# Triangular inverses of a delta-rule attention in other pieces, and their round trip through HBM at other places

## The chip, the cores and the metric

The kernel runs on one core of a Trainium2 chip. The metric is the device time of one execution in microseconds (us). The kernel before took 492.99 us (median of three runs, 492.59 to 494.81).

## What is computed

Two layers. The first is a linear attention with the delta rule, over 4 batches and 8 heads, 768 tokens each, head size 48, all in float32:

```
state = 0                                     # 48 x 48 per batch and head
for t in range(768):
    y[t]  = q[t] @ state
    state = state + beta[t] * outer(k_n[t], v[t] - k_n[t] @ state)     # k_n: k over its norm
```

The second takes the 3072 tokens of width 384 (8 heads of 48), sends each to the best of 8 experts (softmax of a gate, argmax), and multiplies the weight of that expert with `relu(x @ w1[e]) @ w2[e]` (384 to 1024 to 384).

## The kernel before, in words

**Attention, the part that is changed.** The 768 tokens are cut into 6 blocks of 128 (`tb` = 0 to 5). One *item* n = 4 tb + b is block tb of batch b with its 8 heads, so there are 24 items. The program is written as 27 *ticks* t (the loop at L1030): in tick t item t enters, the items t-1 to t-3 move one stage of 32 tokens on, and item t-3 is finished. Every tick has the same steps on TensorE (PE): `residual` (L439, L451), `apply` (L466), `finish` (L489, L500, L509), the products with the queries (`qpart`, L280, tile pq), the Gram matrix of the keys of a later item (`kpart`, L280, tile pg, up to tick 11 only), and the product that hands a finished item to the experts (L533). VectorE (DVE) subtracts the residual (`v_all<-v_all,ks`, L458) once per tick. That instruction stands between `residual` and `apply` of its tick; below, *tick t lasts from the start of L458 of t to that of t+1*.

**Inverses.** The 32 x 32 sub-blocks need, for all 4 batches, 8 heads and 4 stages of a block, the inverse of a unit lower triangular matrix built from the Gram matrix. One 32 x 32 matrix lies on each of 128 partitions, in `lg` (the products) and `lw` (the inverse). DVE does this alone. `prepare` (L310) scales, `lanes` (L362) inverts the two 16 x 16 triangles on the diagonal column by column, c = 1 to 14, with one multiply (L379) and one add (L382) for both triangles at once through a 4-dimensional view (`both_halves`), and then forms the 16 x 16 corner from two products, each as multiply (L398) and reduce (L404) in three pieces of 4, 5 and 7 rows through two buffers `big0` and `big1`. A transpose (L409) gives `wt`, which `apply` of the block's four items reads. The inverse of block 0 stands ahead of tick 0; that of block tb must be done before tick 4 tb, and what is left of it is then put in at one go:

```
while line and line[0].tb <= t // B:
    inverse_step(t)
```

Otherwise the steps of the inverses are strewn over the ticks: each `yield` of `lanes` names a cost in us, and `beside(t, i)`, called seven times a tick, puts in steps up to a budget (`SPEND`, 0.86 to 0.92 us). `ROOT[tb]` gives the places 7t+i at which block tb has its squared norms taken (`squares`, L304, DVE), their square root (`root`, L308, ScalarE, ACT) and at which its inverse may start.

**The round trip.** The Gram of an item lies in `gg` with tokens on partitions; `lg` wants one matrix per partition. So, when the fourth item of a block is through `kpart`, SyncE (SP) stores four slices to HBM (`gd`, L268) and loads the block back as `lg` (L272). For blocks 2 to 5 that is in the middle of tick max(0, 4 tb - 9). SP issues all other loads too, in the order of the program: keys (`kt`, L196), queries, values (`v_all`, L228, L230), and seven clears of the token table in HBM (`xg<-zrow`, L191, 788 KB each, their places set by `CL` and `CLT`). The load of `lg` waits until the stores of `gd` have landed.

**Experts.** From tick 20 on the weights are loaded and split, and behind tick 26 eight experts are computed, on PE at 2.4 GHz almost without a break. This part is not changed.

Of the kernel before, what the change touches and what calls it, by code (L numbers as in the profile page):

```python
# [41 lines left out]
def deltanet_moe(ctx, tc, kt_d, qt_d, kn_d, v_d, beta_d, w_gate, w1, w2, out):  # L42
# [81 lines left out]
    ROOT = {1: (-1, -1, -1), 2: (17, 20, 22), 3: (38, 41, 43), 4: (66, 69, 71), 5: (94, 97, 99)}  # L124
# [9 lines left out]
    CL = (1, (0, 1), (0, 1))  # L134
    CLT = (2, 3, 4, 5)
# [98 lines left out]
    def kpart(n):  # L234
# [28 lines left out]
        if tb > 0 and b == B - 1:  # L263
            early_ = CL[tb] if tb < len(CL) else (0, 0)
            clear_slots(early_[0])
            for i in range(NB):
                r = slice(32 * i, 32 * i + 32)
                nc.sync.dma_start(out=gd[tb].rearrange("(i n) (r c) -> i r n c", i=NB, r=32)[i],  # L268
                                  in_=gg_g[tb % (KSL // B)].rearrange("p b h c -> p (b h) c")[r, :, r])
            tiles[tb]["lg"] = fp.tile([128, 32, 32], F32, name=f"lg{tb}", tag="lg", bufs=3)  # L270
            clear_slots(early_[1])
            nc.sync.dma_start(out=tiles[tb]["lg"].rearrange("p r c -> p (r c)"), in_=gd[tb])  # L272
# [37 lines left out]
    def prepare(tb):  # L310
# [50 lines left out]

    def lanes(tb):  # L362


        T = tiles[tb]
        lg, lw = T["lg"], T["lw"]
        G, W = both_halves(lg), both_halves(lw)
        V = nc.vector
        tmp = fp.tile([128, 128], F32, name=f"tmp{tb}", tag=f"tmp{tb % 2}")
        for c in range(15):  # L370
            m, w = 15 - c, c + 1
            if c == 0:
                for g in (0, 16):
                    V.tensor_scalar(out=lw[:, g + 1:g + 16, g], in0=lg[:, g + 1:g + 16, g], scalar1=lw[:, g, g:g + 1],
                                    scalar2=None, op0=ALU.mult)
                yield 0.4
                continue
# [16 lines left out]
        todo = []  # L394
        for i, (x, y, out, minus) in enumerate(work):
            m, n, k = x.shape[1], y.shape[1], x.shape[2]
            t = big[i % 2][:, 0:m * n * k].rearrange("p (m n k) -> p m n k", m=m, n=n)
            V.tensor_tensor(out=t, in0=x.unsqueeze(2).broadcast_to([128, m, n, k]),  # L398
                            in1=y.unsqueeze(1).broadcast_to([128, m, n, k]), op=ALU.mult)
            yield 0.15 + m * n * k / 960  # L400
            todo.append((out, t, minus))
            while len(todo) > (i not in (2, 5)):
                out, t, minus = todo.pop(0)
                V.tensor_reduce(out=out, in_=t, axis=AX.X, op=ALU.add, negate=minus)  # L404
                yield 0.15 + t.shape[1] * t.shape[2] * t.shape[3] / 960
# [623 lines left out]
    fin = iter(())  # L1029
    for t in range(NN + LAG):  # L1030
# [345 lines left out]
```

## Time and profile before

| what | value |
|---|---|
| median of the runs | 492.99 us |
| profiled execution: time / span | 495.15 us / 493.4 us |
| busy share of the span: PE, DVE, ACT, POOL | 91%, 66%, 54%, 34% |
| the inverse of block 0 on DVE, L341 to L409 | from 12.10 to 36.57 us |
| L458 of tick 0, 12, 20 starts at | 36.42, 140.69, 201.67 us |
| last L458 (tick 26) | 256.06 us |
| mean granted clock of TensorE | 0.975 |

The rows further down come from the profiled execution; times in them count from its span's start. A row of a timeline gives start, length, engine, line, operation, output and inputs with their shapes, the number of instructions merged, and in brackets how long the engine was idle before it and what released it.

### The profile page before, as it was taken

How to read it: one execution, taken by the hardware profiler on the slowest of the kernel's cores; microseconds unless marked ns; L12 is line 12 of the kernel's file. 1: busy time of each engine (PE TensorE's matmuls, PEld its weight loads, DVE VectorE, ACT ScalarE, POOL GpSimd, SP SyncE). 2: the span in 40 equal slices, each digit the busy share in tenths (PEclk: the TensorE clock that was granted, in tenths of full speed). 3: DMA queues.
4: the chain of work that ended last, by engine and by line, in shares of the span. 5: the costliest groups of instructions: out<-in, count | busy, mean ns of one | idle time of the engine just before them, and what ended most of it. 6: DMA issues, size and time to landing. Idle time of an engine off the chain costs nothing. (4 is left out here: it accounts for less than half of the span.)

```text
span 493.4 us, 17242 instructions
## 1 busy us (share of the span) xinstructions
PE 451.3 (91%) x7212; PEld 417.2 (85%) x7212; DVE 326.3 (66%) x728; ACT 264.7 (54%) x580; POOL 166.8 (34%) x342
## 2 busy tenths in 40 slices
PE   6979597989998898987899899999999999999995
PEld 4868486878887777876798899999999999999995
DVE  5999798699999989556543687373563637265230
ACT  4467385667666565777342465463554545364230
POOL 7002142667887878731301210201112020201111
PEclk9698798999999999999999999999999999999999
DMA  8599649667284433635211557374544547353101
GB/s 241 169 273 231 169 95 273 196 131 202 84 169 118 132 107 92 214 126 188 81 55 45 168 171 247 119 217 136 173 142 166 165 160 211 118 177 98 38 1 46
DMA packets 57147, 73.33 MB, mean 149 GB/s; under 512 B 25929, under 2 KB 44831, under 8 KB 57056
## 3 DMA queue, kind: packets, MB, share of 16 engines
q1 hardware_dynamic: 53600, 62.44, 43.7%
q0 software_dynamic: 3456, 9.57, 5.3%
q8 instruction: 71, 1.16, 1.0%
q14 instruction: 20, 0.16, 0.1%
HBM read 54.15 MB, written 18.62 MB: 147 GB/s over the span
## 5 line engine op out<-in xcount | busy, mean ns | idle before, releaser
L808 POOL DMA_INDIRECT out_dram<-yo,idx x32 | 30.8, 963 | 199.3 <-ACT yo L1146 103.5
L805 PE MATMUL y<-w2h,hx 128*128 128x384 f32 x352 | 93.5, 340 | 0.1
L751 DVE TENSOR_TENSOR w2l<-w2r,w2h 128x768 fp32r<-128x768 f32 x32 | 31.2, 979 | 68.8 <-ACT w2h L749 68.7
L805 PEld LDWEIGHTS y<-w2h,hx 128*128 128x128 f32 x352 | 64.1, 188 | 0.4 <-issue 0.4
L805 PE MATMUL y<-w2l,hx 128*128 128x384 f32 x176 | 59.3, 337 | 0.0
L794 PE MATMUL h<-xl,w1h 128*128 128x416 f32 (+2 forms) x168 | 57.3, 341 | 0.2 <-DVE xl L726 0.2
L794 PE MATMUL h<-xh,w1h 128*128 128x416 f32 (+2 forms) x168 | 57.3, 341 | 0.0
L794 PE MATMUL h<-xh,w1l 128*128 128x416 f32 (+2 forms) x168 | 57.2, 341 | 0.0
L470 ACT COPY u<-ks 32x384 f32<-32x384 f32 x96 | 45.1, 470 | 18.3 <-PE ks L466 16.8
L797 ACT ACTIVATE hx<-h 128x448 fp32r<-128x448 f32 (+1 forms) x64 | 32.8, 518 | 31.7 <-PE h L794 31.0
L1146 ACT ACTIVATE yo<-y,gt 128x384 f32<-128x384 f32 x22 | 12.8, 582 | 68.4 <-PE y L805 56.9
L798 DVE SCALAR_TENSOR_TENSOR hx<-h,hx 128x448 fp32r<-128x448 f32 (+1 forms) x64 | 37.1, 587 | 16.2 <-ACT hx L797 16.2
L280 PE MATMUL pg<-kt 64*128 64x128 f32 x384 | 35.9, 315 | 12.8 <-DMA kt<-in_kt_dram 7.2
L291 POOL TENSOR_SCALAR_AFFINE_SELECT pm<-pm 128x1024 f32<-128x1024 f32 x24 | 27.8, 1159 | 51.9 <-ACT pm L290 51.5
L439 PE MATMUL ks<-st,kt 128*32 128x96 f32 x768 | 43.5, 251 | 0.3 <-ACT u L470 0.2
L280 PEld LDWEIGHTS pg<-kt 64*128 64x128 f32 x384 | 30.1, 213 | 16.0 <-DMA kt<-in_kt_dram 6.1
L262 ACT COPY gg<-pg 128x512 f32<-128x512 f32 x48 | 25.7, 587 | 24.9 <-PE pg L280 24.9
L541 POOL DMA_INDIRECT xg<-row,sli x24 | 28.3, 1178 | 23.6 <-ACT yt L513 8.0
L439 PEld LDWEIGHTS ks<-st,kt 128*32 128x32 f32 x768 | 32.6, 110 | 3.9 <-ACT u L470 0.7
L751 DVE TENSOR_TENSOR w1l<-w1r,w1h 128x1024 fp32r<-128x1024 f32 x24 | 29.4, 1223 | 8.9 <-ACT w1h L749 8.9
L466 PE MATMUL ks<-v_all,wt 32*32 32x48 f32 x1536 | 25.0, 205 | 10.5 <-DVE v_all L458 6.3
L466 PEld LDWEIGHTS ks<-v_all,wt 32*32 32x32 f32 x1536 | 21.0, 106 | 14.7 <-DVE v_all L458 8.1
(196 smaller groups left out, 1041.7 us busy)
## 6 DMA issues: line engine op xcount, KB each, us to landing
w1r<-in_w_dram SPq DMA_DIRECT2D x24, 512.0 KB
w2r<-in_w_dram SPq DMA_DIRECT2D x32, 384.0 KB
xg<-zrow SPq DMA_DIRECT2D x7, 788.0 KB
kt<-in_kt_dram SPq DMA_DIRECT2D x17, 256.0 KB
xr<-xg SPq DMA_DIRECT2D x7, 591.0 KB
ku<-in_kn_dram SPq DMA_DIRECT2D x20, 192.0 KB
qt<-in_qt_dram SPq DMA_DIRECT2D x36, 96.0 KB
v_all<-in_v_dram SPq DMA_DIRECT2D x15, 192.0 KB
```

The lines of the kernel that those rows point to most:

```text
L280: nc.tensor.matmul(pg[a][:, p], lhsT=kt[r, p], rhs=xt[r, p], start=True, stop=True, tile_position=(64 * a, 0), skip_group_check=True)
L291: nc.gpsimd.affine_select(out=pm, in_=pm, compare_op=ALU.is_gt, fill=0.0, base=0, pattern=[[0, H], [1, C]], channel_multiplier=-1)
L439: nc.tensor.matmul(ks[32 * q:32 * q + 32, 2 * p:2 * p + 2, :], lhsT=kt_t[n % KTL][:, p, 32 * q:32 * q + 32], rhs=st_view(n % B, p), start= ...
L466: nc.tensor.matmul(ks[r, h, :], lhsT=tiles[n // B]["wt"][r, n % B * H + h, :], rhs=vn[r, h, :], start=True, stop=True, tile_position=(32 * ...
L470: nc.scalar.copy(out=uview(n)[r], in_=ks[r])
L541: put = nc.gpsimd.indirect_dma_start(out=xg, out_offset=bass.IndirectOffsetOnAxis(ap=at, axis=0), in_=x, in_offset=None, bounds_check=OFF ...
L751: nc.vector.tensor_tensor(out=lo[:, j:j + st], in0=raws[k], in1=hi[:, j:j + st].bitcast(F32), op=ALU.subtract)
L794: nc.tensor.matmul(ps, lhsT=w[:, d, fs], rhs=x_[:, d], start=(n == 0), stop=(n == len(terms) - 1))
L797: nc.scalar.activation(out=hh, in_=ps, func=AF.Relu)
L798: nc.vector.scalar_tensor_tensor(out=hl, in0=ps, scalar=0.0, in1=hh.bitcast(F32), op0=ALU.max, op1=ALU.subtract)
L805: nc.tensor.matmul(ps, lhsT=h(f)[h_], rhs=w2[w][:, f, :], start=(n == 0), stop=(n == len(terms) - 1))
L808: nc.gpsimd.indirect_dma_start(out=out, out_offset=bass.IndirectOffsetOnAxis(ap=idx, axis=0), in_=yo, in_offset=None, bounds_check=N - 1, ...
```

## The change

Three parts. (1) In `lanes` each triangle gets a chain of its own: where one multiply and one add did both triangles, there are now two multiplies (one for the matrix at 0, one for that at 16) and then two adds, for c = 1 to 13; the last column is one fused multiply-add per triangle. `prepare` leaves the diagonal and the last column out of its scaling (15 x 15 for 16 x 16). (2) The corner's products come in four pieces of 4 rows each, in the order 0, 1, 3, 2, pieces 1 and 3 side by side in `big1`. The costs that the steps name to the budget are changed with them. (3) For blocks 2 to 5 the stores of `gd` move to the end of their tick, and the load of `lg` to the end of the next tick, ahead of its `load_k`; one clear of `xg` that stood between them moves to the end of tick 1 (`CLT`). `ROOT` lets the blocks start 4 or 5 places later.

```
-    ROOT = {1: (-1, -1, -1), 2: (17, 20, 22), 3: (38, 41, 43), 4: (66, 69, 71), 5: (94, 97, 99)}
+    ROOT = {1: (-1, -1, -1), 2: (22, 25, 27), 3: (42, 45, 47), 4: (70, 73, 75), 5: (98, 101, 103)}
...
-    CL = (1, (0, 1), (0, 1))
-    CLT = (2, 3, 4, 5)
+    CL = (1, (0, 1), (0, 0))
+    CLT = (1, 2, 3, 4, 5)
...
-            x = lg[:, g:g + 16, g:g + 16]
+            x = lg[:, g + 1:g + 16, g:g + 15]
...
-        for c in range(15):
+        for c in range(1, 14):
             m, w = 15 - c, c + 1
-            x = tmp[:, 0:2 * m * w].rearrange("p (g a b) -> p g a b", g=2, a=m)
-            V.tensor_tensor(out=x, in0=G(w, c, m, 1).broadcast_to([128, 2, m, w]),
-                            in1=W(c, 0, 1, w).broadcast_to([128, 2, m, w]), op=ALU.mult)
-            yield 0.2 + m * w / 480
-            V.tensor_tensor(out=W(w, 0, m, w), in0=W(w, 0, m, w), in1=x, op=ALU.add)
-            yield 0.2 + m * w / 480
+            x = [tmp[:, i, 0:m * w].rearrange("p (a b) -> p a b", a=m) for i in range(2)]
+            for i, g in ((0, 0), (1, 16)):
+                V.tensor_tensor(out=x[i], in0=lg[:, g + w:g + 16, g + c:g + w].broadcast_to([128, m, w]),
+                                in1=lw[:, g + c:g + w, g:g + w].broadcast_to([128, m, w]), op=ALU.mult)
+            yield 0.2 + m * w / 700
+            for i, g in ((0, 0), (1, 16)):
+                y = lw[:, g + w:g + 16, g:g + w]
+                V.tensor_tensor(out=y, in0=y, in1=x[i], op=ALU.add)
+            yield 0.2 + m * w / 700
+        for g in (0, 16):
+            y = lw[:, g + 15, g:g + 15]
+            V.scalar_tensor_tensor(out=y, in0=lw[:, g + 14, g:g + 15], scalar=lg[:, g + 15, g + 14:g + 15], in1=y,
+                                   op0=ALU.mult, op1=ALU.add)
...
-        for a, b in ((0, 4), (4, 9), (9, 16)):
-            work.append((first_[:, a:b, a:16], lg[:, 16:32, a:16], prod[:, a:b], False))
-        for a, b in ((12, 16), (7, 12), (0, 7)):
-            work.append((lw[:, 16 + a:16 + b, 16:16 + b], prod[:, :, 0:b], lw[:, 16 + a:16 + b, 0:16], True))
+            for i in (0, 1, 3, 2):
+                a = 4 * i if up else 12 - 4 * i
+                if up:
+                    x, y, out = left[:, a:a + 4, a:16], lg[:, 16:32, a:16], prod[:, a:a + 4]
+                else:
+                    x, y, out = lw[:, 16 + a:20 + a, 16:20 + a], prod[:, :, 0:a + 4], lw[:, 16 + a:20 + a, 0:16]
...
+        if crossing:
+            bounce_in(crossing.pop())
         load_k(t + LEAD + 2)
         if t >= LAG:
             load_q(t - LAG + QTL)
+        for tb in range(2, NT):
+            if t == max(0, B * tb + B - 1 - LEAD):
+                bounce_out(tb)
+                crossing.append(tb)
         clear_slots(CLT.count(t))
```

`bounce_out` holds the four stores of `gd` (L273 in the changed file), `bounce_in` the load of `lg` (L279), both as they were. The columns are L390 and L395 there, the last column L399, the corner L419 and L372.

How the order of instructions moves, at three places. First DVE, at the start of the columns of block 0, before and then after (16 in a row is the pair of scalings of column 0; `x2` marks two instructions alike):

```order
L374 TENSOR_SCALAR lw_153<-lg_292,lw_153 128x15 x2
L379 TENSOR_TENSOR tmp_537<-lg_292,lw_153 128x56
L382 TENSOR_TENSOR lw_153<-lw_153,tmp_537 128x2x14x2
L379 TENSOR_TENSOR tmp_537<-lg_292,lw_153 128x78
L382 TENSOR_TENSOR lw_153<-lw_153,tmp_537 128x2x13x3
```

```order
L383 TENSOR_SCALAR lw_153<-lg_292,lw_153 128x15 x2
L390 TENSOR_TENSOR tmp_537<-lg_292,lw_153 128x28 x2
L395 TENSOR_TENSOR lw_153<-lw_153,tmp_537 128x14x2 x2
L390 TENSOR_TENSOR tmp_537<-lg_292,lw_153 128x39 x2
L395 TENSOR_TENSOR lw_153<-lw_153,tmp_537 128x13x3 x2
```

One instruction for 56 elements became two for 28; the next one no longer needs the one just ahead of it, but the one before that.

Second DVE, the last instructions ahead of L458 of tick 8, before and after (`lw_636` and `lw_666` are the inverse of block 2, `lg_1009` and `lg_1376` the Gram of block 3; L458 is L476 in the changed file):

```order
L404 TENSOR_REDUCE lw_636<-big_2_1461 128x4x16
L341 SCALAR_TENSOR_TENSOR lg_1009<-lg_1009,lw_1122 128x16x16 x2
L349 STREAM_TRANSPOSE r_1452<-s_1451 128x32
L398 TENSOR_TENSOR big_2_1461<-lw_636,lg_677 128x784
L404 TENSOR_REDUCE lw_636<-big_2_1460 128x5x16
L374 TENSOR_SCALAR lw_1122<-lg_1009,lw_1122 128x15 x2
L404 TENSOR_REDUCE lw_636<-big_2_1461 128x7x16
L379 TENSOR_TENSOR tmp_1870<-lg_1009,lw_1122 128x56
L409 STREAM_TRANSPOSE wt_1875<-lw_636 128x32x32
L458 TENSOR_TENSOR v_all<-v_all,ks_1879 128x384
```

```order
L372 TENSOR_REDUCE lw_666<-big_2_1543 128x4x16
L344 TENSOR_TENSOR lw_1141<-ss_1620,r_1622 128x32
L372 TENSOR_REDUCE lw_666<-big_2_1542 128x4x16
L348 SCALAR_TENSOR_TENSOR lg_1376<-lg_1376,lw_1141 128x15x15 x2
L356 STREAM_TRANSPOSE r_1622<-s_1621 128x32
L427 STREAM_TRANSPOSE wt_1927<-lw_666 128x32x32
L476 TENSOR_TENSOR v_all<-v_all,ks_1963 128x384
```

Behind the first reduce shown, a multiply of 784 elements and two reduces were still to come ahead of the transpose, with the first columns of block 3 among them; now one reduce is, and the scaling of block 3.

Third SP, around the load of the keys of item 14 (`kt_135`), which `kpart` needs in tick 2, before and after (`gd_63`, `lg_677` and `lg_897` are block 2):

```order
L196 DMA kt_133<-in_kt_dram 128x512
L196 DMA kt_134<-in_kt_dram 128x512
L105 DMA esel<-in_w_gate_dram 48x2x8 x4
L268 DMA gd_63<-gg_107 32x32x32 x4
L191 DMA xg<-zrow 128x4x394
L272 DMA lg_677<-gd_63 128x1024
L228 DMA v_all<-in_v_dram 32x1536
L196 DMA kt_135<-in_kt_dram 128x512
L228 DMA v_all<-in_v_dram 32x1152
L230 DMA v_all<-in_v_dram 32x384
L196 DMA kt_136<-in_kt_dram 128x512
```

```order
L196 DMA kt_133<-in_kt_dram 128x512
L196 DMA kt_134<-in_kt_dram 128x512
L105 DMA esel<-in_w_gate_dram 48x2x8 x4
L228 DMA v_all<-in_v_dram 32x1536
L196 DMA kt_135<-in_kt_dram 128x512
L273 DMA gd_63<-gg_107 32x32x32 x4
L228 DMA v_all<-in_v_dram 32x1152
L230 DMA v_all<-in_v_dram 32x384
L279 DMA lg_897<-gd_63 128x1024
L196 DMA kt_136<-in_kt_dram 128x512
L191 DMA xg<-zrow 128x4x394
```

The keys of item 14 stood behind the stores of block 2, a clear of 788 KB and the load that waits for the stores; now they stand ahead of all three.

## Rows read from the trace of the kernel before

**Rows 1.** Busy time by stretch; x counts instructions, then PEclk, DMA share, GB/s
```profile
43.97:50.63 6.66, 4.70 (x118) 4.10 (x118) 6.08 (x21) 5.14 (x15) 0.85 (x1) 1.00 0.96 250
50.63:61.57 10.94, 6.70 (x162) 6.03 (x162) 7.40 (x10) 4.40 (x14) 1.39 (x2) 0.69 0.62 159
77.94:89.36 11.42, 8.74 (x232) 7.48 (x231) 7.24 (x23) 6.01 (x15) 3.01 (x11) 0.85 0.87 248
89.36:97.56 8.20, 7.96 (x237) 6.98 (x235) 6.87 (x13) 5.86 (x14) 6.61 (x15) 1.00 0.62 199
97.56:108.36 10.80, 10.02 (x260) 8.74 (x260) 10.22 (x18) 6.85 (x17) 7.05 (x17) 1.00 0.54 103
201.67:208.38 6.71, 6.71 (x217) 5.86 (x217) 2.42 (x6) 5.44 (x13) 5.43 (x15) 1.00 0.75 274
97.56:140.69 43.13, 40.42 (x1180) 35.53 (x1180) 40.54 (x85) 29.36 (x72) 33.56 (x74) 1.00 0.57 138
140.69:201.67 60.98, 54.24 (x1741) 47.32 (x1739) 57.28 (x125) 38.00 (x96) 49.28 (x109) 1.00 0.43 126
36.42:201.67 165.25, 145.31 (x4204) 127.05 (x4202) 148.20 (x330) 107.45 (x275) 105.03 (x227) 0.96 0.58 154
```

**Rows 2.** Timeline of PE: start us, us, instruction, idle before and its releaser
```profile
34.14 0.46 PE L280 MATMUL pg<-kt 64*128 64x128 f32 x2 [1.27 <-DMA kt<-in_kt_dram]
...
35.46 1.16 PE L280 MATMUL pg<-kt 64*128 64x128 f32 x14 [0.86 <-ACT gg L262]
...
54.65 2.08 PE L280 MATMUL pg<-kt 64*128 64x128 f32 x16 [5.92 <-DMA kt<-in_kt_dram]
...
82.84 0.37 PE L466 MATMUL ks<-v_all,wt 32*32 32x48 f32 x4 [2.68 <-issue]
```

**Rows 3.** Timeline of ACT, the square root of block 1
```profile
34.70 0.23 ACT L308 ACTIVATE s<-ss 128x32 f32<-128x32 f32 x1 [2.80 <-DVE ss L304]
```

**Rows 4.** Timeline of SP, the queue that issues loads and stores
```profile
38.12 3.51 SPq L268 DMA_DIRECT2D gd<-gg  x4
41.67 0.80 SPq L191 DMA_DIRECT2D xg<-zrow  x1
45.08 0.34 SPq L272 DMA_DIRECT2D lg<-gd  x1
...
45.94 0.42 SPq L196 DMA_DIRECT2D kt<-in_kt_dram  x1
...
70.80 0.34 SPq L272 DMA_DIRECT2D lg<-gd  x1
```

**Rows 5.** Timeline of DVE, the inverse of block 0
```profile
12.78 0.38 DVE L374 TENSOR_SCALAR lw<-lg,lw 128x15 f32<-128x15 f32 x2
13.19 0.22 DVE L379 TENSOR_TENSOR tmp<-lg,lw 128x56 f32<-128x56 f32 x1
...
16.09 0.29 DVE L379 TENSOR_TENSOR tmp<-lg,lw 128x126 f32<-128x126 f32 x1
16.29 0.20 DVE L349 STREAM_TRANSPOSE r<-s 128x32 f32<-128x32 f32 x1
16.42 0.28 DVE L382 TENSOR_TENSOR lw<-lw,tmp 128x126 f32<-128x126 f32 x1
...
21.38 0.38 DVE L387 COPY lg<-lw 128x256 f32<-128x256 f32 x1
21.79 2.30 DVE L398 TENSOR_TENSOR big<-lg 128x1024 f32<-128x1024 f32 x2
24.00 1.21 DVE L404 TENSOR_REDUCE lg<-big 128x64 f32<-128x1024 f32 x1
...
34.49 0.18 DVE L304 TENSOR_SCALAR ss<-lg 128x32 f32<-128x32 f32 x1
```

**Rows 6.** Timeline of DVE, then of POOL, at one moment of tick 4
```profile
76.84 1.17 DVE L382 TENSOR_TENSOR lw<-lw,tmp 128x128 f32<-128x128 f32 x1
...
76.78 1.09 POOL L291 TENSOR_SCALAR_AFFINE_SELECT pm<-pm 128x1024 f32<-128x1024 f32 x1 [2.94 <-ACT pm L290]
```

More of the change, by code (lines that the diff above doesn't have):

```diff
@@ L262, in kpart, with bounce_out, bounce_in @@
             A(out=gg[:, a:H:2], in_=pg[a])
[L263 to L272, printed above, removed]
+        if tb == 1 and b == B - 1:
+            clear_slots(CL[tb][0])
+            bounce_out(tb)
+            clear_slots(CL[tb][1])
+            bounce_in(tb)
+    def bounce_out(tb):
+        for i in range(NB):
+            r = slice(32 * i, 32 * i + 32)
+            nc.sync.dma_start(out=gd[tb].rearrange("(i n) (r c) -> i r n c", i=NB, r=32)[i],
+                              in_=gg_g[tb % (KSL // B)].rearrange("p b h c -> p (b h) c")[r, :, r])
+    def bounce_in(tb):
+        tiles[tb]["lg"] = fp.tile([128, 32, 32], F32, name=f"lg{tb}", tag="lg", bufs=3)
+        nc.sync.dma_start(out=tiles[tb]["lg"].rearrange("p r c -> p (r c)"), in_=gd[tb])
     def halves(nm, kt, xt):
@@ L339, in prepare @@
         for g in (0, 16):
-            x = lg[:, g:g + 16, g:g + 16]
-            V.scalar_tensor_tensor(out=x, in0=x, scalar=-1.0, in1=diag[:, g:g + 16].unsqueeze(2).broadcast_to([128, 16, 16]),
+            x = lg[:, g + 1:g + 16, g:g + 15]
+            V.scalar_tensor_tensor(out=x, in0=x, scalar=-1.0, in1=diag[:, g + 1:g + 16].unsqueeze(2).broadcast_to([128, 15, 15]),
                                    op0=ALU.mult, op1=ALU.mult)
@@ L360, in both_halves, with summed @@
         return view
+    def summed(todo, which, up):
+        for i in which:
+            out, t = todo[i]
+            nc.vector.tensor_reduce(out=out, in_=t, axis=AX.X, op=ALU.add, negate=not up)
+            yield 0.08 + t.shape[3] / 15
     def lanes(tb):
@@ L366, in lanes @@
         lg, lw = T["lg"], T["lw"]
-        G, W = both_halves(lg), both_halves(lw)
         V = nc.vector
-        tmp = fp.tile([128, 128], F32, name=f"tmp{tb}", tag=f"tmp{tb % 2}")
-        for c in range(15):
-            m, w = 15 - c, c + 1
[L372 to L377, printed above, removed]
-            x = tmp[:, 0:2 * m * w].rearrange("p (g a b) -> p g a b", g=2, a=m)
-            V.tensor_tensor(out=x, in0=G(w, c, m, 1).broadcast_to([128, 2, m, w]),
-                            in1=W(c, 0, 1, w).broadcast_to([128, 2, m, w]), op=ALU.mult)
-            yield 0.2 + m * w / 480
-            V.tensor_tensor(out=W(w, 0, m, w), in0=W(w, 0, m, w), in1=x, op=ALU.add)
-            yield 0.2 + m * w / 480
@@ L394, in lanes @@
[L394 to L405, printed above, removed]
+        tmp = fp.tile([128, 2, 64], F32, name=f"tmp{tb}", tag=f"tmp{tb % 2}")
@@ new lines, in lanes @@
+        for g in (0, 16):
+            V.tensor_scalar(out=lw[:, g + 1:g + 16, g], in0=lg[:, g + 1:g + 16, g], scalar1=lw[:, g, g:g + 1],
+                            scalar2=None, op0=ALU.mult)
+        yield 0.2
+        for c in range(1, 14):
+            m, w = 15 - c, c + 1
+            x = [tmp[:, i, 0:m * w].rearrange("p (a b) -> p a b", a=m) for i in range(2)]
[7 more added lines that the diff above has]
+            yield 0.2 + m * w / 700
@@ new lines, in lanes @@
+        for g in (0, 16):
+            y = lw[:, g + 15, g:g + 15]
+            V.scalar_tensor_tensor(out=y, in0=lw[:, g + 14, g:g + 15], scalar=lg[:, g + 15, g + 14:g + 15], in1=y,
+                                   op0=ALU.mult, op1=ALU.add)
+        yield 0.25
+        big = [fp.tile([128, 1024], F32, name=f"big{i}_{tb}", tag=f"big{i}") for i in range(2)]
+        left, prod = lg[:, 0:16, 0:16], lg[:, 0:16, 16:32]
+        V.tensor_copy(left, lw[:, 0:16, 0:16].rearrange("p k a -> p a k"))
@@ new lines, in lanes @@
+        yield 0.45
+        for up in (True, False):
+            todo = {}
+            for i in (0, 1, 3, 2):
[4 more added lines that the diff above has]
+                    x, y, out = lw[:, 16 + a:20 + a, 16:20 + a], prod[:, :, 0:a + 4], lw[:, 16 + a:20 + a, 0:16]
+                k = x.shape[2]
+                if i == 2:
+                    yield from summed(todo, (0, 1), up)
+                t = big[i % 2][:, 768 * (i == 3):768 * (i == 3) + 64 * k].rearrange("p (m n k) -> p m n k", m=4, n=16)
+                V.tensor_tensor(out=t, in0=x.unsqueeze(2).broadcast_to([128, 4, 16, k]),
+                                in1=y.unsqueeze(1).broadcast_to([128, 4, 16, k]), op=ALU.mult)
+                todo[i] = out, t
+                yield 0.08 + k / 15
+            yield from summed(todo, (3, 2), up)
@@ L1027, in beside @@
             ahead_step()
-    fin = iter(())
+    fin, crossing = iter(()), []
     for t in range(NN + LAG):
@@ L1071, in deltanet_moe @@
             load_q(t - LAG + QTL)
+        for tb in range(2, NT):
+            if t == max(0, B * tb + B - 1 - LEAD):
+                bounce_out(tb)
+                crossing.append(tb)
         clear_slots(CLT.count(t))
```

4 lines of the change are left out of this document (removed).

## The prediction

> **What bounds the kernel now.** I read the busy time by stretch first, then the waits in the timelines of PE, ACT and SP, and last DVE instruction by instruction. Only the stretch up to about 201 us is touched; what follows needs the same work in the same order, so a shift at tick 20 should reach the end unchanged. From the start of tick 0 to that of tick 20 the kernel spends 165.25 us, in which PE is busy 145.31 and DVE 148.20 [rows 1]: neither fills it, so the loss lies in single ticks. An undisturbed tick with `kpart` is tick 6: 8.20 us with PE busy 7.96, which I take as PE's floor for such ticks; without `kpart`, and with DVE nearly idle, tick 20 takes 6.71 us, all of it PE [rows 1]. Against these floors four places stand out.
>
> Ahead of tick 0 DVE works alone at the inverse of block 0. In tick 2 (10.94 us) PE sits idle 5.92 us for the keys of item 14 [rows 1, 2]. Those were issued at 45.94, behind the stores of block 2 (38.12), a clear (41.67) and the load of `lg`, which itself waited until 45.08 for the stores to land [rows 4]. In tick 5 (11.42 us) PE stops 2.68 us in the middle of L466 with nothing released ("issue") and runs on at a mean granted clock of 0.85, that is partly at the lower level of 1.2 GHz [rows 1, 2]. In tick 7 (10.80 us) DVE is busy 10.22: what is left of the inverse of block 2 is put in at one go, and L458 of tick 8 queues behind it [rows 1]. Ticks 7 to 11 take 43.13 us with DVE busy 40.54; ticks 12 to 19 take 60.98 with DVE busy 57.28 against PE 54.24 [rows 1]. There DVE is the nearer bound, so time taken from DVE counts.
>
> **One inverse, on DVE.** An instruction of n elements lasts about 0.16 us + n/960 us (56 elements 0.22, 126 elements 0.29), and one that needs its predecessor starts some 0.035 us after that one's end [rows 5]. What two chains cost is not in the trace, so I bound it. The good end: an instruction that needs only the one before last starts about 0.08 us ahead of its predecessor's end. The reduce at 24.00 is of that kind, it needs the first of the two multiplies, and both end together at 21.79 + 2.30 = 24.09; and the transpose at 16.29, between a multiply and the add that needs it, cost the add nothing (16.42 is 0.04 behind 16.38) [rows 5]. The bad end: no overlap at all. I take the good end, since the rows are of the same engine, type and kind of wait. Columns: 26 pairs, 52 instructions of 0.16 - 0.08 plus 2600 elements, 4.16 + 2.71 = 6.9 us, and 0.4 for the last column, which I price like the two small instructions with a pointer scalar at 12.78 (0.38) [rows 5]. That is 7.3 against 21.38 - 13.19 = 8.19: **-0.9**. Corner: 10240 elements instead of 11072 (-0.87), four more instructions of about 0.075 (+0.3), and the third multiply no longer waits for the first reduce to free its buffer (twice 0.115, -0.23): **-0.8** of 34.49 - 21.79 = 12.70 [rows 5]. The smaller scaling saves 62 elements, 0.06. Together **1.75 us per inverse**, six times, of which only what bounds a tick counts.
>
> Here a rule speaks against the change. The Trainium skill, "VectorE: DVE Perf Modes", section "The DRAIN you can't avoid", says that the next op does not start until the pipeline is empty, whether or not a semaphore is between, with an earlier start only where nothing holds the next op; its "Rules for kernel authors" conclude that one should minimize the op count. By that rule the columns would cost 52 full instructions, and the time would be that of the fourth rival below; the reduce at 24.00, which waits for the instruction before last and yet starts early, does not agree with it.
>
> **Start: -1.2.** DVE reaches L458 of tick 0 about 1.75 us earlier. PE has its own path there: the keys that it needs land at 34.14, then it idles 0.86 us for ACT's copy of a Gram, which stands behind the square root of block 1; that waited 2.80 us for squares which DVE takes behind the inverse [rows 2, 3]. The squares move with the inverse, the 0.86 goes, and PE is through at about 35.75 instead of 36.62. The first `apply` follows the later of the two, so I take 1.2; at least 0.4 (the part of PE's wait that is DVE's alone), at most 1.75.
>
> **Tick 2: -2.9.** The keys of item 14 are now issued behind one load of values, about 38.5 instead of 45.94, with the stores (512 KB), the clear (788 KB) and the load of `lg` (512 KB) behind them instead of ahead. In 38 to 46 these queued for the same transfers, so I expect them some 7 us earlier, near 47, when PE asks for them. What is late next is DVE: it was busy 7.40 in this tick, and its order now puts about half a microsecond more of block 1 there, so the tick becomes 8.0. The stores of block 2 still wait for ACT's copy of item 11, but what stands behind them is now due a tick later: the keys of item 15 follow the load of `lg` and have until tick 3. The load itself has to land ahead of the squares in tick 3, over a tick later.
>
> **Tick 5: -2.4.** SP stood still until the load of block 3 at 70.80 [rows 4] and then issued the queued loads and two clears in a burst, at a DMA share of 0.87 [rows 1]. Now nothing waits in front of them, and the load of `lg` only meets stores that left a tick ago. I expect the stop to go (3.1, from 11.42 to 8.3) but cannot show that the burst caused it, so I count three quarters; zero if not.
>
> **Ticks 7 to 11: -1.7.** The order ahead of L458 of tick 8 holds one reduce less and no big multiply. Five ticks at PE's floor are 41.0; I take 41.4, since the work moves into ticks 9 and 10, where DVE stays close to PE. Zero at worst, 2.1 at best.
>
> **Ticks 12 to 19: -2.4.** Two inverses, 3.5 us of DVE; in part PE's own work shows instead (its floor is 8 x 6.71 = 53.7, so there is room), and where the preparation of the next block is interleaved, the waits between dependent instructions were hidden already. Between 0 and 3.5.
>
> ROOT's later places and POOL's clearing of `lw` cost nothing as far as the order tells: the square root still stands ahead of ACT's copies for the experts, and the squares just behind L458. If that cover were gone, ACT would stand as in the row at 34.70.
>
> **Sum:** 1.2 + 2.9 + 2.4 + 1.7 + 2.4 = 10.6 against the profiled execution's 495.15 gives 484.5. The profiled execution lies 2.2 above the median of 492.99, and nearly all of that could be the stop in tick 5; the sum without tick 5 against the median, 492.99 - 8.2, is 484.8, so the two ways agree.
>
> **The rivals.**
> - *The keys are late anyhow.* The DMA engines, not SP's order, set the arrival. For it: their share is 0.96 in tick 1 [rows 1]. Against: the bytes ahead of the keys shrink by 1.8 MB. Tick 2 would keep 2.9, so 487.5.
> - *POOL takes it back.* In tick 4 an add that met a masking of POOL lasted 1.17 instead of 0.29 us [rows 6]. Shorter chains spread over more ticks could meet six more of the 24 maskings: 6 x 0.88 = 5.3, so about 489.5. Against: the multiplies and adds take less of DVE's time than before, not more.
> - *DVE was not the bound.* Only SP's order counts, and the clumps appear elsewhere: about 492.
> - *No overlap (slower).* If every instruction of the columns pays its full length, they cost 52 x 0.195 + 2.71 = 12.9 us instead of 7.7 without the last, so an inverse gets 4.3 us longer. The first shows in full, and five more put 21.5 on DVE's 148.20, more than the 17.05 in which it is idle; with part of the ticks' idle time used up, some 10 us in the ticks and 4.3 ahead of them: 507. It decides below an overlap of about 0.065 us, where two short instructions cost as much as one long one. That is not far from 0.08, but the rows at 24.00 and 16.29 stand against it.
>
> **How the numbers follow.** Forecast 0.60, late keys 0.15, POOL 0.12, no gain 0.08, slower 0.05. The forecast's own range is 481 to 488 (the terms at their better ends give 14; without tick 5, 487). 480.5 to 490 takes in the first two rivals and leaves out some 15 in 100. A measurement of this kernel tells about 0.5%, 2.5 us, from no change: faster is below 490.5, the forecast, late keys and three quarters of POOL, 0.84; same 0.11; slower 0.05.
>
> **What would show it.** L458 of tick 0 near 35; column pairs of 0.23 to 0.29 us; no wait of PE for `kt` in tick 2; no DVE tick above 9 us; tick 20 near 191. Wrong would be a pitch between the two chains equal to their length, PE idle for keys in tick 2 or 3, DVE idle ahead of L304, or ticks 12 to 19 still at 61 us.

## The result, and the profile after

Over 19 runs of each the changed kernel took a median of 487.21 us (483.04 to 491.09), the kernel before 494.3: a ratio of 0.987 with a 95% interval of 0.984 to 0.989 (a ratio here and below leaves out the few runs that lie over 1.5% above the fastest of their kernel). It is faster, by 7.1 us where 8.5 were forecast (484.5 against 492.99), and inside the range of 480.5 to 490. The profiled execution took 483.36 us, 3.85 below its own median, so its rows show more gain (11.8) than the medians do. The busy time by stretch, for the changed kernel, in the stretches of [rows 1] (ticks 1, 2, 5, 6, 7, then 7 to 11 and 12 to 19):

```profile
42.58:49.94 7.36, 6.77 (x106) 6.16 (x108) 7.33 (x32) 4.10 (x13) 1.48 (x2) 0.54 0.82 195
49.94:57.50 7.56, 6.22 (x176) 5.32 (x174) 7.53 (x12) 5.88 (x17) 1.30 (x3) 0.99 0.87 282
73.38:81.48 8.10, 7.10 (x229) 6.12 (x229) 7.54 (x31) 5.77 (x14) 4.33 (x10) 1.00 0.83 266
81.48:89.67 8.19, 7.99 (x237) 7.07 (x234) 7.68 (x15) 5.99 (x15) 7.03 (x15) 1.00 0.67 208
89.67:97.85 8.18, 7.84 (x237) 6.87 (x237) 6.83 (x16) 5.77 (x14) 6.62 (x18) 1.00 0.43 141
89.67:130.63 40.96, 39.47 (x1173) 34.58 (x1173) 34.66 (x115) 29.16 (x71) 31.02 (x75) 1.00 0.56 151
130.63:190.90 60.27, 54.92 (x1749) 47.86 (x1745) 56.96 (x187) 38.05 (x97) 47.37 (x109) 1.00 0.43 123
```

Tick 0 starts at 35.00 instead of 36.42, tick 20 at 190.90 instead of 201.67. Tick 2 fell from 10.94 to 7.56, tick 5 from 11.42 to 8.10, tick 7 from 10.80 to 8.18. DVE's busy time in ticks 7 to 11 fell from 40.54 to 34.66, but in ticks 12 to 19 only from 57.28 to 56.96. The later ROOT is a small part of that shift: root_old (below), the changed kernel with the earlier ROOT, has 35.88 and 56.79 in the same two stretches:

```profile
94.90:136.75 41.85, 39.42 (x1168) 34.64 (x1169) 35.88 (x114) 29.15 (x71) 30.20 (x72) 1.00 0.57 149
136.75:202.26 65.51, 56.57 (x1749) 49.30 (x1748) 56.79 (x180) 38.04 (x97) 48.34 (x111) 0.97 0.41 115
```

The mean granted clock of tick 2 is 0.99 for 0.69, that of tick 1 0.54 for 1.00, nearly all of it at 1.2 GHz, and tick 1 is 0.7 longer.

The timeline of DVE, start of the inverse of block 0, and of SP in ticks 0 and 1, both of the changed kernel:

```profile
13.40 0.32 DVE L390 TENSOR_TENSOR tmp<-lg,lw 128x28 f32<-128x28 f32 x2
13.64 0.31 DVE L395 TENSOR_TENSOR lw<-lw,tmp 128x28 f32<-128x28 f32 x2
...
16.48 0.36 DVE L390 TENSOR_TENSOR tmp<-lg,lw 128x64 f32<-128x64 f32 x2
16.76 0.36 DVE L395 TENSOR_TENSOR lw<-lw,tmp 128x64 f32<-128x64 f32 x2
...
20.32 0.39 DVE L405 COPY lg<-lw 128x256 f32<-128x256 f32 x1
```

```profile
38.31 0.35 SPq L196 DMA_DIRECT2D kt<-in_kt_dram  x1
39.11 3.68 SPq L273 DMA_DIRECT2D gd<-gg  x4
...
45.37 0.34 SPq L279 DMA_DIRECT2D lg<-gd  x1
45.77 1.08 SPq L196 DMA_DIRECT2D kt<-in_kt_dram  x1
```

The columns take 20.32 - 13.40 = 6.92 us (8.19 before, 7.3 forecast). The keys of item 14 are issued at 38.31, where 45.94 stood [rows 4], and PE has no wait for keys in tick 2.

The waits of PE in ticks 0 to 19 (for what, us in total, times, longest), changed kernel; "issue" stands for a stop in which the profile shows nothing that PE waited for:

```profile
PE ks L484 <- DVE v_all L476: 4.3, 4, 1.3
PE sum L518 <- ACT u L488: 2.2, 8, 0.3
PE ks L484 <- issue: 2.1, 2, 1.1
PE pp L689 <- POOL oh_all L685: 1.6, 2, 0.9
```

### The profile page after: what moved, and what is told of

Its sections match the earlier page's. It is cut to its first block, busy times and chain, and to the rows that moved or that the text cites. A ratio compares the mean times of both kernels' runs of the same rounds, so it can differ in the third digit from the quotient of the medians.

```text
span 481.6 us, 17425 instructions
## 1 busy us (share of the span) xinstructions
PE 450.5 (94%) x7212; PEld 416.1 (86%) x7212; DVE 320.3 (66%) x908; ACT 264.8 (55%) x580; POOL 164.3 (34%) x342
## 5 line engine op out<-in xcount | busy, mean ns | idle before, releaser
L812 PE MATMUL h<-xl,w1h 128*128 128x416 f32 (+2 forms) x168 | 57.3, 341 | 0.2 <-DVE xl L744 0.2
L812 PE MATMUL h<-xh,w1l 128*128 128x416 f32 (+2 forms) x168 | 57.3, 341 | 0.0
L812 PE MATMUL h<-xh,w1h 128*128 128x416 f32 (+2 forms) x168 | 57.3, 341 | 0.0
L457 PE MATMUL ks<-st,kt 128*32 128x96 f32 x768 | 44.6, 254 | 0.7 <-ACT u L488 0.7
L298 POOL TENSOR_SCALAR_AFFINE_SELECT pm<-pm 128x1024 f32<-128x1024 f32 x24 | 26.6, 1109 | 38.9 <-ACT pm L297 38.3
L559 POOL DMA_INDIRECT xg<-row,sli x24 | 27.0, 1123 | 23.5 <-ACT yt L531 8.0
L823 PEld LDWEIGHTS y<-w2l,hx 128*128 128x128 f32 x176 | 33.1, 188 | 0.0
```

Source lines behind the costliest of these rows:

```text
L298: nc.gpsimd.affine_select(out=pm, in_=pm, compare_op=ALU.is_gt, fill=0.0, base=0, pattern=[[0, H], [1, C]], channel_multiplier=-1)
L457: nc.tensor.matmul(ks[32 * q:32 * q + 32, 2 * p:2 * p + 2, :], lhsT=kt_t[n % KTL][:, p, 32 * q:32 * q + 32], rhs=st_view(n % B, p), start= ...
L559: put = nc.gpsimd.indirect_dma_start(out=xg, out_offset=bass.IndirectOffsetOnAxis(ap=at, axis=0), in_=x, in_offset=None, bounds_check=OFF ...
L812: nc.tensor.matmul(ps, lhsT=w[:, d, fs], rhs=x_[:, d], start=(n == 0), stop=(n == len(terms) - 1))
L823: nc.tensor.matmul(ps, lhsT=h(f)[h_], rhs=w2[w][:, f, :], start=(n == 0), stop=(n == len(terms) - 1))
```

## The experiments

Three sets of kernels ran, each beside the kernel before on one chip; its medians there were 493.83, 493.89 and 496.71, so ratios are what compares across sets.

### Which part carries the gain

Five mixtures of the three parts. "New inverses" are the two chains, the corner in four pieces and the smaller scaling (its first row and last column are left out); these three were not run apart from each other. The old round trip with the old inverses and the late ROOT was not run either.

| kernel | round trip | ROOT | inverses | median us | ratio to before (95%) |
|---|---|---|---|---|---|
| bounce_only | new | late | old | 496.60 | 1.007 (1.004 to 1.011) |
| bounce_rootold | new | early | old | 492.01 | 0.993 (0.990 to 0.997) |
| inv_only | old | early | new | 495.24 | 1.000 (0.996 to 1.004) |
| inv_rootnew | old | late | new | 491.29 | 0.993 (0.990 to 0.996) |
| root_old | new | early | new | 493.75 | 0.999 (0.995 to 1.002) |
| the change, again (first set) | new | late | new | 489.04 | 0.989 (0.983 to 0.995) |
| the change, third time (third set) | new | late | new | 491.00 | 0.989 (0.986 to 0.992) |

**bounce_only** keeps the old `lanes` and the 16 x 16 scaling in the changed kernel, **inv_only** puts the new ones into the kernel before:

> Only the stores and loads of the Gram squares, the clear and ROOT are moved, the inverses stay as they were. Theory (SP's order and DVE's work each give a part): PE no longer waits for keys in tick 2, that tick falls from 10.9 to about 8 us and tick 5 loses its stop in some runs, but L458 of tick 0 stays at about 36.5 and the clumps of the inverses stay in some ticks: 490 us, 3.5 to 5 below before. Rival (SP's order alone did it): as fast as the changed kernel, 487. Rival (DVE alone did it): within 1 us of before, 494.

> Only the inverses are changed, the round trip through HBM, the clears and ROOT stay where they were. Theory: L458 of tick 0 at about 35, tick 7 without its clump, but PE still waits some 5 us for keys in tick 2: 490.5 us, 3 to 4.5 below before. Rival (SP's order alone did it): 493 to 494. Rival (DVE alone did it): 487.

Neither half gains alone; one loses. No theory had that. bounce_only has tick 2 at 6.87, as wanted, but ticks 7 and 15 are worse than before: all DVE, the rest of an inverse put in at one go (windows of its ticks 7 and 15):

```profile
92.43:104.15 11.72, 10.07 (x260) 8.82 (x260) 11.72 (x23) 7.50 (x18) 7.68 (x17) 1.00 0.60 139
159.18:171.11 11.93, 7.99 (x228) 6.83 (x227) 11.90 (x20) 5.36 (x14) 9.45 (x23) 1.00 0.29 89
```

That put the blame on ROOT, the edit that the prediction had costed at nothing. Three more mixtures undo or do it:

```
-    ROOT = {1: (-1, -1, -1), 2: (22, 25, 27), 3: (42, 45, 47), 4: (70, 73, 75), 5: (98, 101, 103)}
+    ROOT = {1: (-1, -1, -1), 2: (17, 20, 22), 3: (38, 41, 43), 4: (66, 69, 71), 5: (94, 97, 99)}
```

> The changed kernel with the old inverses and the old ROOT: only the round trip through HBM is new. Theory A (the later ROOT is a loan that only the shorter inverse can pay: with the old one the rest that is put in at one go ahead of ticks 8, 12 and 16 grows): without the later ROOT the loss of the round trip alone goes, tick 2 near 7, ticks 7 and 15 back at 10.1 to 10.8 instead of 11.7 and 11.9, median about 490. Theory B (PE's stops behind late packets of instructions set the difference, wherever the inverses stand): about 495, with ticks 5 and 6 at 9.5 or more each. Theory C (the round trip's new place is itself harmful): as with the later ROOT, about 496.5.

> The changed kernel with the old, earlier ROOT. Theory A: the shorter inverse does not need the later start and loses little by the earlier one, 487 to 489, with ticks 12 and 16 a little shorter and ticks 7 to 11 a little longer. Theory B: as the changed kernel, 487 to 490, since ticks 5 and 6 are the same. A rival to both (the later ROOT is what brings the gain): 491 or more, and the squares wait for the load of lg, so that DVE is idle ahead of L311.

> The kernel before with the new inverses and the new ROOT: only the round trip is the old one. Theory A (the loan is paid, only the wait for keys in tick 2 and what follows from it are left): tick 2 near 10.8, the other ticks as in the changed kernel, about 490.5, which is 3 above the changed kernel. Theory B (SP's burst behind the load of lg makes PE's instructions late in ticks 5 and 6 whatever DVE does): about 494, as the new inverses alone with the old ROOT.

With the old inverses and the new round trip the later start loses 1.4% (0.993 to 1.007), as theory A said: in bounce_rootold ticks 7 and 15 are back at 10.85 and 10.16. With the new ones it gains 1.0% (0.999 to 0.989) or 0.7% (1.000 to 0.993), which A had wrong for root_old; the third theory had its time (491 or more), but not its sign: for blocks 2 to 5, whose places ROOT moves, DVE does not idle ahead of L311 (it does, 1.61 us, for block 1 ahead of tick 0). In inv_rootnew tick 2 keeps its wait for keys (timeline of PE, tick 2):

```profile
53.83 2.08 PE L280 MATMUL pg<-kt 64*128 64x128 f32 x16 [6.28 <-DMA kt<-in_kt_dram]
```

So the change is two gains of about 0.7% each, the round trip's and that of the inverses *with* their ROOT, and the pair of them adds up (0.993 x 0.993 = 0.986). Without the later ROOT the new inverses gain nothing, with the old round trip (1.000) or the new one (0.999).

### What the early ROOT costs the new inverses

In root_old PE waits elsewhere than in the changed kernel: 6.5 us for `oh_all`, POOL's part of the routing, instead of 1.6. The waits of PE in its ticks 0 to 19:

```profile
PE ks L484 <- DVE v_all L476: 7.7, 7, 2.3
PE pp L689 <- POOL oh_all L685: 6.5, 5, 3.4
```

The timelines of POOL (ticks 7 and 15) and of PE (tick 16) of root_old:

```profile
95.40 0.22 POOL L360 COPY nt_all<-r 32x32 f32<-32x32 f32 x1
98.11 1.18 POOL L360 COPY nt_all<-r 32x32 f32<-32x32 f32 x3 [2.49 <-DMA xg<-row,sli]
...
163.02 0.99 POOL L559 DMA_INDIRECT xg<-row,sli  x1 [0.17 <-issue]
164.00 0.25 POOL L360 COPY nt_all<-r 32x32 f32<-32x32 f32 x1
167.85 0.69 POOL L360 COPY nt_all<-r 32x32 f32<-32x32 f32 x3 [3.60 <-issue]
...
171.50 0.26 POOL L685 TENSOR_SCALAR oh_all<-oh 128x16 bf16<-128x16 f32 x1
```

```profile
171.81 0.17 PE L689 MATMUL pp<-oh_all,ltri 128*128 128x16 bf16 x1 [3.42 <-POOL oh_all L685]
```

POOL copies the norms of a new block (L360) in four pieces. In tick 7 the profile names what the second piece waits for: the landing of a scatter of rows. In tick 15 the scatter stands right ahead of the copies, the second piece starts 3.60 us late, and the routing behind it, and PE, are late with it; tick 16 takes 11.25 us. In the changed kernel the copies stand behind the routing and a masking, and run at one go:

```profile
160.28 1.09 POOL L298 TENSOR_SCALAR_AFFINE_SELECT pm<-pm 128x1024 f32<-128x1024 f32 x1 [0.80 <-ACT pm L297]
161.32 0.95 POOL L360 COPY nt_all<-r 32x32 f32<-32x32 f32 x4
```

In tick 11 the second piece waits 1.93 us, and there too the profile names the scatter. To test whether this wait is what the early ROOT costs, **norms3** takes root_old and moves the norms of blocks 2 to 5 behind the third column:

```
@@ prepare
-        if tb > 0:
-            yield from norms(tb)
@@ norms, its end
-        yield
+        yield 0.0
@@ lanes, ahead of the columns
+        if tb == 1:
+            yield from norms(tb)
@@ lanes, in the loop over c
+            if tb > 1 and c == 3:
+                yield from norms(tb)
```

> The changed kernel with the old, earlier ROOT (493.75 us), but with the transpose and the four copies of the norms (L356, L360) put behind column 3 of the inverse, so that POOL's copies no longer stand right behind a scatter of rows. Theory D (what the old ROOT costs together with the new inverses is one wait: POOL's second copy waits 2 to 3.6 us for the landing of the scatter issued just ahead of it, the routing chain queues behind it, and PE waits for oh_all): POOL's copies run in one go of about 0.95 us, PE waits for oh_all less than 0.5 us in all where it was 0.85, 0.45, 0.76 and 3.42, tick 16 falls from 11.25 to 9 or less, median 488 to 490. Theory A (the later start of the inverses itself brings the gain, by where the rest of the inverse and POOL's maskings fall): 492 to 494, tick 16 still above 10.

The time did not fall: 496.35 us, ratio 1.000 (0.997 to 1.003), where the changed kernel on the same chip has 0.989. Waits of PE for `oh_all` in ticks 0 to 19, and its ticks 15 and 16:

```profile
PE pp L691 <- POOL oh_all L687: 1.8, 2, 1.1
```

```profile
158.00:167.03 9.03, 8.05 (x215) 6.69 (x214) 6.04 (x17) 4.78 (x12) 5.18 (x13) 0.81 0.36 115
167.03:175.57 8.54, 8.06 (x228) 6.98 (x225) 8.54 (x48) 4.79 (x12) 6.94 (x20) 1.00 0.32 97
```

Most of the wait went (6.5 to 1.8, against under 0.5 expected) and tick 16 fell by 2.7, but tick 15 is 9.03 (8.08 in root_old) at a lower clock, and tick 20 takes 10.49 with a stop of PE of 1.69. So theory D has its wait and not its price. The edit also moved block 1 and the order on DVE (tick 0 starts at 34.09, tick 1 lasts 8.24), so it does not change the wait alone. What the later ROOT is worth, 3.5 to 5 us, lies in ticks 12 to 19: they take 65.51 us in root_old and 64.36 in norms3, but 60.27, 59.89 and 61.65 in three profiles of the changed kernel; and 64.56 in inv_only, but 60.57 in inv_rootnew. The mean granted clock there is 0.97 in the three kernels with the early ROOT and 1.00 in the others. What causes it stays open.

### What two chains are worth

**in_line** issues the chains one behind the other, so that each add follows its own multiply; the same instructions and the same elements:

```
-            yield 0.2 + m * w / 700
-            for i, g in ((0, 0), (1, 16)):
-                y = lw[:, g + w:g + 16, g:g + w]
-                V.tensor_tensor(out=y, in0=y, in1=x[i], op=ALU.add)
-            yield 0.2 + m * w / 700
+                y = lw[:, g + w:g + 16, g:g + w]
+                V.tensor_tensor(out=y, in0=y, in1=x[i], op=ALU.add)
+                yield 0.2 + m * w / 700
```

> The changed kernel with its two chains put one behind the other: multiply and add of the first triangle, then of the second, the same instructions, each add right behind the multiply that it needs. Theory (what two chains gain is the overlap of neighbours that do not need each other): 26 adds wait about 0.1 us more, so the columns of block 0 take 9 to 10 us instead of 6.9, L458 of tick 0 is at about 37.5, and the time is 490 to 492. Rival (each instruction pays its full length anyhow, and the gain came from elsewhere): columns unchanged, 487.

It took 504.67 us, ratio 1.022 (1.016 to 1.028): 15.6 slower than the changed kernel in the same set, and worse than any theory said. The timeline of DVE at its first columns, and the waits of PE in ticks 0 to 19:

```profile
13.64 0.18 DVE L390 TENSOR_TENSOR tmp<-lg,lw 128x28 f32<-128x28 f32 x1
13.85 0.19 DVE L393 TENSOR_TENSOR lw<-lw,tmp 128x28 f32<-128x28 f32 x1
13.96 0.18 DVE L390 TENSOR_TENSOR tmp<-lg,lw 128x28 f32<-128x28 f32 x1
```

```profile
PE ks L482 <- DVE v_all L474: 15.9, 8, 3.4
PE pp L687 <- POOL oh_all L683: 3.4, 3, 1.7
```

An add that needs the multiply just ahead starts 0.03 us behind its end (13.82, 13.85); the next multiply, which needs nothing, starts 0.08 ahead of the add's end (14.04, 13.96). That is the pair of numbers the prediction took from [rows 5]. The columns with the last one take 9.91 us instead of 6.92. Six times 3.0 is 18, of which 15.6 reached the end: nearly nine tenths of what was added to DVE was paid.

### PE's stops in ticks 5 and 6

The same program, profiled again:

> The changed kernel itself, beside the others on one chip and with another profiled execution: 487 us, 6 to 8 below before. Its profiled execution should show which ticks differ between executions of one program: by the first trace the ticks where PE stops without a releaser, and those with PE at a lower clock; if so ticks 0 to 6 differ and ticks 7 to 11 stay at 8.2.

> The changed kernel a third time, beside the three others on the same chip: 486 to 490 by every theory. Its profile tells which ticks are the same in every execution (all from 7 on, within 0.3 us) and which are not (ticks 2, 5 and 6, by PE's stops without a releaser and the granted clock behind them, by theory B).

489.04 and 491.00 us. Ticks 5 and 6 together took 16.29 in the first profile, 21.22 and 19.20 in these (19.62 before). The windows of both ticks of the second and then of the third profile:

```profile
75.41:86.97 11.56, 9.66 (x237) 8.41 (x237) 7.64 (x30) 5.86 (x14) 5.25 (x12) 0.85 0.81 257
86.97:96.63 9.66, 8.19 (x237) 7.09 (x235) 7.66 (x14) 6.19 (x15) 7.15 (x15) 1.00 0.39 118
```

```profile
72.48:81.57 9.09, 7.29 (x229) 6.15 (x229) 7.55 (x31) 5.78 (x14) 4.87 (x10) 1.00 0.89 286
81.57:91.68 10.11, 8.19 (x237) 7.08 (x235) 7.67 (x14) 6.19 (x15) 6.75 (x14) 1.00 0.48 149
```

So the stop of tick 5 was not removed; the first profile of the changed kernel merely has little of it (1.00 us). From tick 7 on the first two profiles agree to 0.4 us per tick up to 19; the third does not (tick 14 takes 8.45 for 6.91), against what was expected.

What the stops are: the program's instructions come in through DMA queues of their own (the page lists "q8 instruction", 71 packets of 16 KB). By the records of those packets in the traces:

```
profile        packet starts after the one before   landed   PE goes on   stop
before                     6.3 us                    81.37      82.84      2.68
the change                 5.9                       74.84      76.27      1.00
again                      6.1                       78.66      80.18      1.90
again                      8.2                       90.64      92.01      1.47
bounce_only                5.9                       86.52      87.81      1.65
```

In the 14 profiles of this case there are 21 stops without a releaser ("issue") of 0.8 us or more in ticks 5 and 6, and each ends 1.2 to 1.6 us behind the landing of such a packet; 17 of those packets started 5.5 us or more after the one before, where 4 to 5 is usual further on. A late packet alone does not make a stop, though: in ticks 0 to 4 and 7 to 19 of the same profiles 79 packets started that late, and behind 73 of them PE has no such stop of even 0.4 us. The fourth of the table (DMA view of the second profile): from 82.7 to 89.6 there is no such packet at all while loads fill the engines, and in the next 1.1 us there is one and almost nothing else.

```profile
DMA packets 975, 1.59 MB, mean 231 GB/s; under 512 B 111, under 2 KB 751, under 8 KB 975
...
q1 hardware_dynamic: 975, 1.59, 72.3%
```

```profile
DMA packets 2, 0.02 MB, mean 15 GB/s; under 512 B 1, under 2 KB 1, under 8 KB 1
...
q8 instruction: 1, 0.02, 5.5%
```

If loads make them late, fewer loads there should help. **clear_t2** and **early3** clear the token table earlier:

```
-    CLT = (1, 2, 3, 4, 5)
+    CLT = (1, 2, 2, 3, 5)      (clear_t2)
+    CLT = (1, 2, 2, 2, 3)      (early3)
```

> The changed kernel with two clears of the token table earlier: those at the ends of ticks 3 and 4 move to the ends of ticks 2 and 3, where the DMA engines are idle from 56 to 60 us; 788 KB less in the crowded stretch from 70 to 84 us. Theory B (a packet of PE's instructions that meets the burst lands late, and PE stops): the stops in ticks 5 and 6 shrink from 3.4 us in the second profile of the changed kernel to under 1, median 484 to 486. Theory A: no part of it, the same as the changed kernel, 487 to 489. A rival (the clear delays keys or values in ticks 3 and 4): 490 or more, with a wait of PE for kt or of DVE for v_all there.

> The changed kernel with the clears from the ends of ticks 3, 4 and 5 at the ends of ticks 2, 2 and 3: two of 788 KB leave the stretch from 70 to 86 us, where the DMA engines are full, for that from 51 to 60, where they are nearly idle. Theory B (PE's instructions come late where their packet meets a full stretch): PE's stops without a releaser in ticks 5 and 6 together under 1 us and both ticks at 8.2 to 8.5, median 2 to 4 below the changed kernel of the same call, 483.5 to 485.5. Its rival (the stops come with PE's own place in its instructions, whatever the DMA engines do): stops of 1 to 3.4 us as in the changed kernel, the same median within 1 us.

clear_t2: 486.38 us, ratio 0.985 (0.981 to 0.990); its profile still has a stop of 1.91 in tick 5, where under 1 was expected. early3: 489.81, ratio 0.989 (0.984 to 0.994), the same as the changed kernel in its set. Windows of its ticks 2, 3, 5 and 6:

```profile
49.50:57.96 8.46, 5.26 (x160) 4.47 (x160) 8.43 (x11) 5.24 (x15) 1.86 (x3) 1.00 1.05 344
57.96:66.16 8.20, 7.61 (x212) 6.71 (x213) 6.18 (x13) 5.95 (x19) 0.95 (x1) 0.79 0.52 158
...
74.00:82.91 8.91, 8.25 (x237) 7.03 (x237) 7.67 (x30) 5.78 (x14) 5.49 (x12) 1.00 0.73 196
82.91:91.57 8.66, 8.38 (x237) 7.24 (x235) 7.71 (x14) 6.09 (x15) 7.31 (x15) 1.00 0.35 99
```

In early3 ticks 5 and 6 are 1.6 us shorter than in the third profile (17.57 for 19.20), with stops of only 0.66 and 0.28; ticks 2 and 3 are 1.5 longer (16.66 for 15.20). So theory B has the stops of this one profile and not the total. That the loss moved with the bytes is not shown: ticks 2 and 3 take 16.36 in the second profile of the changed kernel, with the clears at their old places, and ticks 5 and 6 took 16.29 in its first. Neither kernel is shown to beat the change.

Last, **load_at_once** puts the load of `lg` behind its stores again, at the tick's end:

```
                 bounce_out(tb)
-                crossing.append(tb)
+                bounce_in(tb)
```

> The changed kernel with the load of lg right behind its stores again, still at the tick's end: only the load's tick of delay is undone. If the delay matters (SP stands until the stores have landed and everything behind it is issued in a burst): DVE or PE wait for values or keys in ticks 2 to 5, ticks 4 and 5 grow by 2 to 3, and the median is 490 or more. If it does not (all of the round trip's gain is that the stores moved behind the keys of their tick): as the changed kernel, 487 to 489, tick 2 at 8.5 or less.

493.64 us, ratio 0.994 (0.991 to 0.998) against 0.989 for the changed kernel: the tick of delay is worth some 2.6 us, give or take 1.6. Without it little is left of the round trip's gain, since inv_rootnew, with the old round trip, has 0.993. Where the 2.6 us lie is not clear: tick 2 is the same (7.56), tick 4 did not grow (8.36), and ticks 5 and 6 take 10.94 and 9.29, 1.0 more than in the third profile of the changed kernel. DVE's waits of over 1 us in ticks 1 to 6 are for PE and for ACT's square root, none for values.

## Why the prediction was right, point by point

It was right in sign and inside its range; how near the number came is in part luck. Tick 20 starts 10.8 us earlier in the first profile, where 10.6 was forecast, but 4.1 and 6.6 earlier in the other two, and the medians differ by 7.1. The terms, against [rows 1], in the three profiles of the changed kernel:

| term | forecast | first | again | third |
|---|---|---|---|---|
| start of tick 0 | -1.2 | -1.4 | -0.5 | -1.6 |
| tick 2 | -2.9 | -3.4 | -2.5 | -3.4 |
| ticks 5 and 6 (forecast for 5) | -2.4 | -3.3 | +1.6 | -0.4 |
| ticks 7 to 11 | -1.7 | -2.2 | -2.0 | -1.4 |
| ticks 12 to 19 | -2.4 | -0.7 | -1.1 | +0.7 |
| start of tick 20 | -10.6 | -10.8 | -4.1 | -6.6 |

On the mean of the three profiles the start, tick 2 and ticks 7 to 11 gave 6.1 us (5.8 forecast), and the other two terms 1.1 (4.8 forecast). The first profile hides that with a tick 5 that the same program does not repeat. Nor does a shift at tick 20 reach the end unchanged, as the prediction took it: of the third profile's 6.6 us the span kept 3.9, with tick 22 at 11.21 us where it was 8.42.

- **One inverse: right, and more.** Forecast 1.75 us: columns 0.9 (measured 1.27: 52 instructions in 6.63 us for 6.9, the last column 0.29 for 0.4), corner 0.8 (0.86: 11.92 for 12.78, from the first multiply to the end of the last reduce). The overlap of 0.08 read at 24.00 [rows 5] is there in in_line's rows, and the rival without overlap (507) falls: the changed kernel has 180 more instructions on DVE (908 for 728) and 6.0 us less busy time (320.3 for 326.3). With it falls the rule of the Trainium skill ("VectorE: DVE Perf Modes", "The DRAIN you can't avoid", that the next op waits for the empty pipeline) as the prediction read it. The same section of the Trainium skill adds: "A next op that is not held starts earlier". The trace agrees with that, by 0.08 us, so the page did not rule the change out. The nearest thing to the rival that could be built, in_line, pays 504.67.
- **Start: right, with a new limit.** The prediction named DVE idle ahead of L304 as a sign of being wrong. It came, at block 1: DVE now asks for that block's Gram before its load has landed. The wait (L304 is L311 here) is 0.43, 1.38 and 0.27 us in the three profiles and none before, and explains why the second gains only 0.5. First and second profile:

```profile
33.09 0.19 DVE L311 TENSOR_SCALAR ss<-lg 128x32 f32<-128x32 f32 x1 [0.43 <-DMA lg<-gd]
```

```profile
34.03 0.19 DVE L311 TENSOR_SCALAR ss<-lg 128x32 f32<-128x32 f32 x1 [1.38 <-DMA lg<-gd]
```

- **Six times 1.75 is 10.5, and DVE's busy time fell by 6.0.** Busy time is the wrong measure here, as it leaves out the short waits inside a dependent chain. With the gaps of up to 0.15 us between neighbours counted in, DVE is taken for 184.8 us up to tick 20 before and for 174.2 in the first profile: 10.6 less. But 2.9 of this are instructions that POOL no longer holds up (last point). Of the other 7.7 the first inverse has 2.1, which leaves the other five some 1.1 each. Why they give less stays open: the hidden waits that the prediction named do not explain it, since in the kernel before 61 of their 70 adds stood right behind their own multiply.
- **Tick 2: right.** The old round trip with new inverses waits 6.51 (inv_only) and 6.28 us (inv_rootnew) for the keys; the changed kernel waits for none in its three profiles. The rival of late keys falls. How much of the tick's gain the whole kernel keeps is less clear, since load_at_once, with the same tick 2, has 0.994.
- **Tick 5: the mechanism was wrong.** "I expect the stop to go": it went in none of the three profiles, which have stops of 1.00 us, 1.90 us, and 1.00 plus 0.80 us in tick 5 where it was 2.68, and two of them 1.47 and 1.93 us in tick 6. With SP unblocked the DMA engines are as full in tick 5 as before (0.83, 0.81 and 0.89 for 0.87). The prediction had said that it could not show the cause; counting three quarters of it was too much.
- **Ticks 12 to 19: the term that failed.** The forecast took 3.5 us off DVE there and 2.4 off the ticks; in the third profile they take 61.65, which the prediction had named as a sign of being wrong. With the short gaps counted in, DVE lost 1.9 there (59.2 to 57.3) and 6.6 in ticks 7 to 11 (41.3 to 34.7), which could use only 2.2 of it: PE is busy 39.47 of their 40.96 us. ROOT is not the main reason: with the earlier one (root_old) the two figures are 56.9 and 35.9. The heap of tick 15 (10.11) went to ticks 12 (8.20, all DVE) and 16 (8.62).
- **"ROOT's later places cost nothing": wrong, in both directions.** They cost the old inverses 1.4% and are worth 0.7 to 1.0% to the new ones, without which these gain nothing. That the forecast held although this edit was priced at nothing is luck. The cover that was named (ACT and the squares) held; what the prediction left out was POOL, where the place of the norms' copies against the scatters sets a wait of PE (norms3 removed most of that wait and no time), and the ticks at each block's boundary.
- **POOL takes it back: no, it gives some.** Instructions on DVE that take over 0.4 us more than the median of their kind, like the one of [rows 6], are 7 in the first profile against 11 before, 6.2 us over it in all against 9.1. In ticks 7 to 11 there were four, 3.2 us over, each beside a masking (L291) of POOL; the changed kernel has none there in any of its three profiles. The prediction had no term for that. One of the four (its kind takes 0.27), kernel before:

```profile
114.44 1.58 DVE L379 TENSOR_TENSOR tmp<-lg,lw 128x110 f32<-128x110 f32 x1
```

## What to carry to other kernels

A dependent chain of short instructions is cheaper as two interleaved chains, even at twice the count, where the engine lets a neighbour that waits for nothing start early; read that from the trace for the kind of instruction at hand. Busy time leaves out the short waits inside such a chain, so count them in when you price it. A table that sets when work starts is tuned to that work's length: change both together and try each alone, or the one that was "free" hides the gain. Before counting a stop without a releaser as removable, look at a second profile of the same program.

## What was not expected of the hardware

PE's stops without a releaser ended 1.2 to 1.6 us behind the landing of a packet of the program's own instructions, 21 times out of 21. Small copies on POOL waited 1.9 to 3.6 us for the landing of the scatter ahead of them (named as the releaser in ticks 7 and 11 of root_old, read from their place in tick 15). And the stretch at the lower clock did not go with the wait for keys: before, ticks 0 and 2 have a mean granted clock of 0.77 and 0.69; in the three profiles of the changed kernel it is tick 1 (0.54), tick 3 (0.78) and tick 0 (0.60).
